# Another opening, another order of small moves and another order of the last stores in a chunked attention kernel with a fused feed-forward

## The chip, the cores and the metric

One core of one Trainium2 chip. The metric is the device time of one execution, in microseconds. Each time is a median or mean over several executions, and what is read from a profile is of one execution; only runs in the fast state (granted TensorE clock 0.993 to 1.00) are compared. In the profile, PE is TensorE's products, PEld its weight loads, DVE is VectorE, ACT is ScalarE, POOL is GpSimd and SP is SyncE, which here only issues transfers.

## The reference

```python
def _attn_ref(q, k, v):                     # each (8, 8, 576, 64), float32
    ...                                     # chunks of 64 positions
    scores = scale * np.matmul(q_c, k_c.transpose(0, 1, 2, 4, 3))
    scores = scores - np.max(scores, axis=-1, keepdims=True)
    attn = np.exp(scores)
    attn = attn / (np.sum(attn, axis=-1, keepdims=True) + 1e-09)
    out = np.matmul(attn, v_c)
    return out.reshape(B, H, S, D)

def _moe_ref(x, w1, w2, w3, w_out):         # x: the attention output as (4608, 512)
    a = x @ w1                              # 512 x 1024
    b = x @ w2
    h = a * b @ w3                          # 1024 x 1024
    return h @ w_out                        # 1024 x 512
```

## The kernel before

The kernel is a list of steps, one letter each, in the order in which they are recorded. A *pair* is 256 tokens (18 pairs in all). For pair p: `q k v` load (GpSimd issues, cast to bf16 on the way), `T` transposes q or k on VectorE, `S` makes scores, `E` is the exponential on ScalarE, `P` the value products, `N` and `X` normalise and transpose on VectorE, `A` and `B` are the products with w1 and w2, `C` copies A's result out on ScalarE, `M` multiplies on VectorE. `V`, `W`, `Z` turn w3 and w_out into one matrix; `O`, `Y`, `Q` are the last product, its copy and its store. `i0` to `i3` are four column pieces of w1 and w2, `o` is w_out, `h0 h1` are the halves of w3. `D` issues products with zeros: `D0.1.4.512` is four of 512 columns. A load such as `q0` is a whole tile of 256 KB in bf16, `q0.0` the half of it with the first half of the heads.

```python
ORDER = """
q0.0 k0.0 q0.1 k0.1 v0 q1.0 q1.1 k1.0 k1.1 i0 v1 q2 k2 i1 v2 i2 i3 q3 k3 v3 o h0 h1 q4 k4 v4
D0.0.32.64 T0.0.0 T0.1.0 T0.0.1 S0.0 T0.1.1 q5 k5 v5 E0.0 S0.1 E0.1 P0.0 P0.1 T1.0.0 N0.0 T1.1.0
...                                          # cut
O16 Y15 Q15 O17 Y16 Q16 Y17 Q17
"""

def do_G(g, a):                              # regroups transposed q and k: qkm <- qkT, 4 moves of 128 KB, 8 for a group
    ...
    for i in (2 * a, 2 * a + 1):
        for e in range(2):
            move(qkm_t[g][blk[2 * a + e], i % 2], qkT_t[g][blk[i], e])

def do_H(g, a):                              # the same for the normalised output: xt <- xm, 64 KB each
    xt = new_xt(g)[:].rearrange("p (s c) -> p s c", s=2)
    for k_ in range(2):
        for i in (2 * a, 2 * a + 1):
            move(xt[blk[2 * a + k_], i % 2], xm_t[g][blk[i], k_].rearrange("p o m t -> p (o m t)"))

def do_O(p):
    if p < NP - 1:
        ...                                  # both halves of the pair; copied by Y, stored by Q
        return
    ...                                      # the last pair: copied and stored in three parts here
```

`move` and the stores are transfers on SyncE's one queue, in program order; `blk[i]` is the i-th group of 32 partitions.

The softmax here doesn't subtract the row's maximum and nothing guards it: scores larger than these inputs give would overflow.

Of the kernel before, what the change touches and what calls it, by code (L numbers as in the profile page):

```python
# [7 lines left out]

ORDER = """
q0.0 k0.0 q0.1 k0.1 v0 q1.0 q1.1 k1.0 k1.1 i0 v1 q2 k2 i1 v2 i2 i3 q3 k3 v3 o h0 h1 q4 k4 v4  # L10
D0.0.32.64 T0.0.0 T0.1.0 T0.0.1 S0.0 T0.1.1 q5 k5 v5 E0.0 S0.1 E0.1 P0.0 P0.1 T1.0.0 N0.0 T1.1.0
T1.0.1 S1.0 T1.1.1 q6 k6 v6 E1.0 X0.0 S1.1 N0.1 X0.1 P1.0 E1.1 T2.0 A0.0 T2.1 q7 k7 B0.0 C0.0 P1.1
v7 M0.0 A0.1 N1.0 B0.1 C0.1 X1.0 S2 N1.1 E2 M0.1 X1.1 P2 A1.0 N2.0 B1.0 X2.0 C1.0 A1.1 N2.1 B1.1
M1.0 C1.1 X2.1 A2.0 M1.1 B2.0 C2.0 A2.1 M2.0 B2.1 T3.0 C2.1 A0.2 M2.1 B0.2 C0.2 T3.1 q8 k8 v8 A1.2
M0.2 B1.2 C1.2 S3 M1.2 A2.2 E3 B2.2 C2.2 P3 M2.2 A0.3 N3.0 B0.3 X3.0 C0.3 A1.3 N3.1 B1.3 M0.3 C1.3
X3.1 A2.3 M1.3 B2.3 C2.3 A3.0 M2.3 B3.0 V0 C3.0 A3.1 M3.0 B3.1 V1 C3.1 A3.2 M3.1 B3.2 C3.2 V2 A3.3
M3.2 B3.3 C3.3 V3 W0 M3.3 T4.0 W1 Z0 V4 V5 T4.1 q9 k9 v9 W2 Z1 V6 V7 T5.0 S4 Z2 W3 T5.1 q10 k10 E4
T6.0 T6.1 P4 v10 q11 k11 Z3 S5 N4.0 O0 E5 X4.0 N4.1 X4.1 T7.0 O1 T7.1 Y0 Q0 T8.0 P5 v11 q12 k12 Y1
S6 T8.1 O2 Q1 E6 N5.0 X5.0 N5.1 X5.1 O3 T9.0 T9.1 Y2 G4.0 P6 v12 q13 k13 A4.0 N6.0 B4.0 G4.1 Y3 X6.0
N6.1 C4.0 A4.1 X6.1 B4.1 C4.1 M4.0 Q2 S7 Q3 M4.1 A4.2 E7 T10.0 B4.2 C4.2 T10.1 P7 v13 q14 k14 A4.3  # L20
M4.2 B4.3 N7.0 C4.3 A4.4 X7.0 M4.3 B4.4 C4.4 N7.1 A4.5 M4.4 B4.5 C4.5 X7.1 S8 M4.5 S9 E8 A4.6 T11.0
B4.6 E9 T11.1 P8 v14 q15 k15 C4.6 A4.7 M4.6 G5.0 B4.7 C4.7 N8.0 A6.0 M4.7 B6.0 N8.1 C6.0 G5.1 A6.1
X8.0 B6.1 M6.0 C6.1 X8.1 P9 v15 q16 k16 A6.2 M6.1 N9.0 B6.2 C6.2 N9.1 A6.3 M6.2 B6.3 C6.3 X9.0 A6.4
M6.3 B6.4 C6.4 X9.1 A6.5 T12.0 H4.0 B6.5 C6.5 M6.4 A6.6 M6.5 B6.6 T12.1 H4.1 C6.6 S10 S11 M6.6 E10
A6.7 T13.0 B6.7 E11 P10 v16 q17 k17 T13.1 C6.7 O4 M6.7 G6.0 N10.0 N10.1 X10.0 G6.1 P11 v17 Y4 X10.1
O5 N11.0 N11.1 Q4 X11.0 X11.1 T14.0 A8.0 H5.0 Y5 B8.0 T14.1 C8.0 A8.1 M8.0 B8.1 H5.1 C8.1 T15.0 A8.2
B8.2 M8.1 C8.2 T15.1 Q5 A8.3 B8.3 C8.3 M8.2 G7.0 S12 M8.3 S13 E12 A8.4 T16.0 B8.4 E13 G7.1 P12 T16.1
C8.4 A8.5 B8.5 M8.4 C8.5 N12.0 A8.6 M8.5 B8.6 C8.6 N12.1 A8.7 M8.6 B8.7 C8.7 X12.0 P13 M8.7 A10.0
X12.1 B10.0 C10.0 N13.0 A10.1 M10.0 B10.1 N13.1 C10.1 A10.2 X13.0 B10.2 M10.1 C10.2 X13.1 S14 S15
M10.2 E14 A10.3 H6.0 T17.0 B10.3 E15 P14 T17.1 C10.3 A10.4 H6.1 M10.3 B10.4 C10.4 N14.0 A10.5 M10.4  # L30
B10.5 G8.0 C10.5 N14.1 A10.6 M10.5 B10.6 C10.6 X14.0 P15 G8.1 X14.1 A10.7 M10.6 B10.7 N15.0 C10.7 O6
N15.1 M10.7 X15.0 X15.1 H7.0 S16 Y6 S17 O7 E16 E17 H7.1 P16 Y7 O8 Q6 N16.0 Q7 N16.1 X16.0 X16.1 P17
Y8 A12.0 N17.0 Q8 B12.0 N17.1 C12.0 A12.1 X17.0 B12.1 M12.0 C12.1 X17.1 A12.2 M12.1 H8.0 B12.2 C12.2
A12.3 M12.2 B12.3 C12.3 H8.1 A12.4 M12.3 B12.4 C12.4 A12.5 M12.4 B12.5 C12.5 A12.6 M12.5 B12.6 C12.6
A12.7 M12.6 B12.7 C12.7 O9 M12.7 O10 Y9 Q9 A14.0 Y10 B14.0 C14.0 Q10 A14.1 M14.0 B14.1 C14.1 A14.2
M14.1 B14.2 C14.2 A14.3 M14.2 B14.3 C14.3 A14.4 M14.3 B14.4 C14.4 A14.5 M14.4 B14.5 C14.5 A14.6
M14.5 B14.6 C14.6 A14.7 M14.6 B14.7 C14.7 O11 M14.7 O12 Y11 Q11 A16.0 Y12 B16.0 C16.0 Q12 A16.1
M16.0 B16.1 C16.1 A16.2 M16.1 B16.2 C16.2 A16.3 M16.2 B16.3 C16.3 A16.4 M16.3 B16.4 C16.4 A16.5
M16.4 B16.5 C16.5 A16.6 M16.5 B16.6 C16.6 A16.7 M16.6 B16.7 C16.7 O13 M16.7 O14 Y13 Q13 O15 Y14 Q14
O16 Y15 Q15 O17 Y16 Q16 Y17 Q17  # L40
"""


# [1 line left out]
def kernel(  # L45
# [11 lines left out]
    nc = tc.nc  # L57
    B, H, S, D = q.shape
    P = 128
    BL = 32  # L60
    NB = P // BL
    CH = 64
# [14 lines left out]
    bf = mybir.dt.bfloat16  # L77
    f32 = mybir.dt.float32
# [4 lines left out]
    io = ctx.enter_context(tc.tile_pool(name="io", bufs=2))  # L83
    asb = ctx.enter_context(tc.tile_pool(name="asb", bufs=2))
    msb = ctx.enter_context(tc.tile_pool(name="msb", bufs=2))
    ps = ctx.enter_context(tc.tile_pool(name="ps", bufs=4, space=bass.MemoryType.PSUM))

    def inorder(ins):
        tc.keep_in_program_order(ins)
        return ins  # L90
# [35 lines left out]
    qk_t = {}  # L126

    HH = H // 2

    def heads(h):  # L130
        return slice(0, H) if h is None else slice(h * HH, (h + 1) * HH)

# [29 lines left out]
    blk = [slice(i * BL, (i + 1) * BL) for i in range(NB)]  # L162
    qkT_t, qkm_t, s_t, e_t, pv_t, xn_t, xm_t, xt_t = {}, {}, {}, {}, {}, {}, {}, {}
# [4 lines left out]
    def move(dst, src):  # L168
        inorder(nc.sync.dma_start(dst, src))
# [11 lines left out]
    def do_G(g, a):  # L181

        if a == 0:
            qkm_t[g] = asb.tile([P, 2, 2, 2, H, CH], bf, tag="qkm", bufs=2, name="qkm")
        for i in (2 * a, 2 * a + 1):
            for e in range(2):
                move(qkm_t[g][blk[2 * a + e], i % 2], qkT_t[g][blk[i], e])

    def do_S(p, hh=None):
        g, m = divmod(p, 2)  # L190
# [50 lines left out]
    def new_xt(g):  # L241

        if g not in xt_t:
            xt_t[g] = asb.tile([P, KO * GT], bf, tag="xt", bufs=4, name="xt")
        return xt_t[g]
# [18 lines left out]
    def do_H(g, a):  # L264

        xt = new_xt(g)[:].rearrange("p (s c) -> p s c", s=2)
        for k_ in range(2):
            for i in (2 * a, 2 * a + 1):
                move(xt[blk[2 * a + k_], i % 2], xm_t[g][blk[i], k_].rearrange("p o m t -> p (o m t)"))

    ab_t, ps_t, a_t, o_t = {}, {}, {}, {}

# [115 lines left out]
    def load_half3(i):  # L388
# [5 lines left out]



    do = {"q": load_q, "k": load_k, "v": load_v, "i": load_w12, "o": load_wo, "h": load_half3, "T": do_T, "S": do_S, "E": do_E, "G": do_G, "H": do_H,
          "P": do_P, "N": do_N, "X": do_X, "A": do_A, "B": do_B, "C": do_C, "M": do_M, "D": do_D, "V": do_V,
          "W": do_W, "Z": do_Z, "O": do_O, "Y": do_Y, "Q": do_Q}
    for step in ORDER.split():  # L400
# [31 lines left out]
```

## Time and profile before

| | before |
|---|---|
| median | 250.58 us |
| span in the profile | 249.3 us |
| TensorE busy | 226.9 us |
| first product with w1 starts | 19.48 us |
| VectorE's last copy starts | 244.40 us |

The page gives busy times as shares of the span, then one digit of busy tenths per fortieth of it; the chain that ended last is followed back from the last instruction. The lines on which the argument stands are in the prediction below. The first load stream in stretches of 3 us (stretch, its length, then PE, PEld, DVE, ACT and POOL busy with counts, granted clock, DMA share, GB/s), of the kernel before:

```profile
6.00:9.00 3.00, 1.08 (x64) 0.94 (x64) 2.19 (x3) 0.60 (x1) 3.00 (x6) 1.00 1.77 130
9.00:12.00 3.00, 1.23 (x80) 0.90 (x72) 0.78 (x2) 0.60 (x1) 3.00 (x5) 1.00 1.64 158
12.00:15.00 3.00, 0.56 (x32) 0.50 (x32) 2.09 (x5) 0.00 (x0) 2.58 (x5) 1.00 1.38 156
```

### The profile page before, as it was taken

To read this page: it belongs to the slowest core of one execution; us is meant where nothing else is said; L and a number is where in the kernel's file an instruction comes from. 1 tells how busy PE (TensorE), PEld (TensorE's weight loads), DVE (VectorE), ACT (ScalarE), POOL (GpSimd) and SP (SyncE) were. 2 spreads that over 40 slices of the span, in tenths; PEclk is the share of its full clock that TensorE was granted. 3 is DMA by queue.
4 is the path that set the end of the run, shared out by engine and by line. 5 is a ranking of instruction groups with operands and counts; after the bars stand their busy time and mean duration, and the time that the engine had idled before them with its cause. 6 is when DMAs were issued, how large, how long until landed. Compare 5 with 4: busy or idle time off the path is not lost.

```text
span 249.3 us, 6372 instructions
## 1 busy us (share of the span) xinstructions
PE 226.9 (91%) x2740; PEld 122.0 (49%) x2760; DVE 154.5 (62%) x236; ACT 83.4 (33%) x116; POOL 86.9 (35%) x116
## 2 busy tenths in 40 slices
PE   3328899999999999999999999999999999999992
PEld 2225688874455445444444444444444444444441
DVE  2566965899879588999998798918440331233000
ACT  2110324332343333535335325262332332331322
POOL 8977854486997254573660000000000000000000
PEclk9999999999999999999999999999999999999998
DMA  7999999999999999999999974635502200400334
GB/s 67 145 165 182 193 185 201 196 174 172 155 169 209 221 225 249 177 209 193 204 194 235 271 128 99 147 76 199 151 3 84 84 0 9 162 0 1 139 116 168
DMA packets 93660, 37.12 MB, mean 149 GB/s; under 512 B 77120, under 2 KB 86592, under 8 KB 93632
## 3 DMA queue, kind: packets, MB, share of 16 engines
q0 software_dynamic: 84736, 19.41, 84.6%
q1 hardware_dynamic: 8896, 17.31, 24.0%
q8 instruction: 22, 0.36, 0.6%
q14 instruction: 6, 0.05, 0.1%
HBM read 38.80 MB, written 9.44 MB: 194 GB/s over the span
## 4 chain that ended last, share of the span: by engine, by line
PE 73%; DMA 17%; POOL 3%; DVE 2%; issue 1%; ACT 1%; SPq 0%; DVEq 0%; ACTq 0%; POOLq 0%
PE ab_ps L93 41%; PE o_ps L93 22%; DMA out_dram<-o_sb 6%; DMA w<-in_moe_w_dram 6%; PE w_ps L93 6%; DMA qkm<-qkT 5%; PE s_ps L93 3%; PE pv L93 2%; POOL qk L96 2%; DVE qkT L177 1%; POOL vbuf L96 1%; ACT e L209 0%; DVE ab L321 0%; POOL w L96 0%; ACT a_sb L306 0%
## 5 line engine op out<-in xcount | busy, mean ns | idle before, releaser
L93 PE MATMUL ab_ps<-xt,w 128*128 128x512 bf16 (+1 forms) x697 | 130.0, 343 | 1.1 <-DMA w<-in_moe_w_dram 0.5
L93 PEld LDWEIGHTS <-w 128*128 128x128 bf16 x704 | 67.8, 99 | 55.6 <-DMA w<-in_moe_w_dram 0.9
L321 DVE TENSOR_TENSOR ab<-a_sb,ab_ps 128x512 bf16<-128x512 f32 x72 | 48.9, 679 | 49.3 <-ACT a_sb L306 49.2
L306 ACT COPY a_sb<-ab_ps 128x512 f32<-128x512 f32 x72 | 42.2, 585 | 87.9 <-PE ab_ps L93 85.9
L93 PE MATMUL o_ps<-w3o,ab 128*128 128x512 bf16 (+1 forms) x285 | 63.3, 373 | 0.6
L177 DVE STREAM_TRANSPOSE qkT<-qk 128x1024 bf16<-128x1024 bf16 (+1 forms) x40 | 45.6, 1178 | 11.0 <-DMA qk<-in_q_dram 8.3
L93 PEld LDWEIGHTS <-ab 128*128 128x128 bf16 x296 | 28.5, 98 | 32.2
L96 POOL DMA_DIRECT2D vbuf<-in_v_dram x40 | 33.8, 854 | 14.6 <-DMA qk<-in_q_dram 6.4
L351 ACT COPY o_sb<-o_ps 128x1024 f32<-128x1024 f32 x17 | 17.2, 1012 | 42.8 <-PE o_ps L93 38.8
L239 DVE TENSOR_TENSOR xn<-pv,rc 128x512 bf16<-128x512 f32 x36 | 24.9, 692 | 1.2
L96 POOL DMA_DIRECT2D qk<-in_k_dram x26 | 20.2, 782 | 10.0 <-DMA vbuf<-in_v_dram 7.3
L96 POOL DMA_DIRECT2D qk<-in_q_dram x26 | 20.3, 788 | 8.2 <-DMA qk<-in_k_dram 2.3
L209 ACT ACTIVATE e<-s_ps 128x1024 bf16<-128x1024 f32 (+1 forms) x18 | 17.1, 978 | 8.9 <-PE s_ps L93 8.7
L93 PE MATMUL pv<-vbuf,e 64*32 64x65 bf16 (+1 forms) x832 | 11.0, 200 | 4.5 <-DMA vbuf<-in_v_dram 3.3
L93 PE MATMUL w_ps<-wo,w3T 128*128 128x512 bf16 x62 | 14.0, 379 | 0.1
L93 PEld LDWEIGHTS <-e 64*32 64x32 bf16 (+1 forms) x832 | 8.3, 99 | 11.5 <-issue 6.6
L236 DVE RECIPROCAL rc<-pv 128x8 f32<-128x8 f32 x36 | 6.9, 192 | 11.3 <-PE pv L93 11.2
L96 POOL DMA_DIRECT2D w<-in_moe_w_dram x16 | 11.1, 696 | 7.4 <-DMA wo<-in_moe_w_out_dram 3.4
L259 DVE STREAM_TRANSPOSE xm<-xn 128x512 bf16<-128x512 bf16 x20 | 13.6, 697 | 0.2
L251 DVE STREAM_TRANSPOSE xt<-xn 128x512 bf16<-128x512 bf16 x16 | 11.3, 707 | 0.4
L93 PEld LDWEIGHTS <-qkT 32*64 32x64 bf16 x512 | 5.8, 116 | 11.2 <-DVE qkT L177 9.2
L344 DVE COPY o_sb<-o_ps 128x256 f32<-128x256 f32 x1 | 0.4, 424 | 16.0 <-PE o_ps L93 16.0
(19 smaller groups left out, 45.4 us busy)
## 6 DMA issues: line engine op xcount, KB each, us to landing
out_dram<-o_sb SPq DMA_DIRECT2D x17, 512.0 KB, 2.9
qkm<-qkT SPq DMA_DIRECT2D x40, 128.0 KB, 7.2
vbuf<-in_v_dram POOLq DMA_DIRECT2D x32, 128.0 KB, 8.7
w<-in_moe_w_dram POOLq DMA_DIRECT2D x16, 256.0 KB, 10.0
qk<-in_q_dram POOLq DMA_DIRECT2D x10, 256.0 KB, 8.3
qk<-in_k_dram POOLq DMA_DIRECT2D x10, 256.0 KB, 10.1
xt<-xm SPq DMA_DIRECT2D x40, 64.0 KB, 3.0
qk<-in_q_dram POOLq DMA_DIRECT2D x8, 128.0 KB, 5.1
```

Of the source, the lines that this page charges most:

```text
L93: return inorder(nc.tensor.matmul(*a, **kw))
L96: return inorder(nc.gpsimd.dma_start(dst, src))
L177: inorder(nc.vector.transpose(qkT_t[g][:, :, p % 2, s, heads(h)].rearrange("p e h (y t) -> p h t e y", t=2), qk_t[p][:, s, heads(h)].rearr ...
L209: inorder(nc.scalar.activation(e_t[p][:, :, heads(hh)], s_t[p][:].rearrange("p u (h q) -> p u h q", q=CH)[:, :, heads(hh)], Exp, scale=sca ...
L236: inorder(nc.vector.reciprocal(rc[:], pv[:, :, :, D:W]))
L239: inorder(nc.vector.tensor_mul(xn_t[p][:, u], pv[:, :, :, 0:D], rc.to_broadcast([P, 2, 4, D])))
L251: inorder(nc.vector.transpose(new_xt(g)[:].rearrange("p (o t) -> p o t", o=KO)[:, :, t0:t0 + UT] .rearrange("p o (m y) -> p m o y", y=BL), ...
L259: inorder(nc.vector.transpose(xm_t[g][:, u, :, m].rearrange("p o (c y) -> p c o y", y=BL), xn_t[p][:].rearrange("p u r m d -> p (u r) m d" ...
L306: inorder(nc.scalar.copy(a_t[p, j][:], ps_t[p, j][:, 0, :]))
L321: inorder(nc.vector.tensor_mul(o, view(a_t.pop((p, j))[:]), view(ps_t.pop((p, j))[:, 1, :])))
L344: inorder(copy(o_sb[:, u, n0:n1], t[:, 0, 0:n1 - n0]))
L351: inorder(nc.scalar.copy(o_sb[:], ps_t.pop(p)[:]))
```

## The change

Its intent: TensorE's first expert products earlier and at the rate of the later ones (110 ns each instead of 205); the small moves spread over both halves of the partitions; the big store of pair 16 out of the way of the very last one. `R` loads half of pair 0's q as fp32 on the queue of SyncE or of ScalarE (the two hardware queues of the prediction), and `K` casts it on ScalarE; all other loads up to pair 4 are whole tiles now.

```diff
 ORDER:
-q0.0 k0.0 q0.1 k0.1 v0 q1.0 q1.1 k1.0 k1.1 i0 v1 q2 k2 i1 v2 i2 i3 q3 k3 v3 o h0 h1 q4 k4 v4
-D0.0.32.64 T0.0.0 T0.1.0 T0.0.1 S0.0 T0.1.1 ...
+R0 R1 k0 v0 q1 i0 k1 v1 i1 i2 q2 k2 v2 i3 q3 k3 v3 q4 k4 v4 o h0 h1 D0.0.16.64 K0 K1 T0.0 T0.1 q5 k5
+v5 S0 T1.0 E0 P0 D0.1.4.512 T1.1 q6 k6 v6 N0.0 S1 D1.0.5.512 X0.0 N0.1 X0.1 A0.0 E1 B0.0 C0.0 P1
 ... (A to M of pairs 0 to 3 in another order; scores of pair 4 ahead of A3.0)
-O16 Y15 Q15 O17 Y16 Q16 Y17 Q17
+O16 Y15 Q15 Y16 Q16 O17

+    def do_R(h):
+        raw_t[h] = msb.tile([P, HH, 2 * D], f32, tag="o_sb", name="raw")
+        inorder((nc.sync, nc.scalar)[h].dma_start(raw_t[h][:], q[0, heads(h), 0:4 * CH, :]...))
+    def do_K(h):
+        ...
+        inorder(nc.scalar.copy(qk_t[0][:, 0, heads(h)], raw_t[h][:]))

 do_G:
-        for i in (2 * a, 2 * a + 1):
-            for e in range(2):
-                move(qkm_t[g][blk[2 * a + e], i % 2], qkT_t[g][blk[i], e])
+        for i in (0, 2, 1, 3):
+            e = (i + a) % 2
+            move(qkm_t[g][blk[i // 2 * 2 + e], i % 2], qkT_t[g][blk[i], e])
 do_H: likewise
```

More of the change, by code (lines that the diff above doesn't have):

```diff
@@ L9 @@
 ORDER = """
-q0.0 k0.0 q0.1 k0.1 v0 q1.0 q1.1 k1.0 k1.1 i0 v1 q2 k2 i1 v2 i2 i3 q3 k3 v3 o h0 h1 q4 k4 v4
-D0.0.32.64 T0.0.0 T0.1.0 T0.0.1 S0.0 T0.1.1 q5 k5 v5 E0.0 S0.1 E0.1 P0.0 P0.1 T1.0.0 N0.0 T1.1.0
-T1.0.1 S1.0 T1.1.1 q6 k6 v6 E1.0 X0.0 S1.1 N0.1 X0.1 P1.0 E1.1 T2.0 A0.0 T2.1 q7 k7 B0.0 C0.0 P1.1
-v7 M0.0 A0.1 N1.0 B0.1 C0.1 X1.0 S2 N1.1 E2 M0.1 X1.1 P2 A1.0 N2.0 B1.0 X2.0 C1.0 A1.1 N2.1 B1.1
-M1.0 C1.1 X2.1 A2.0 M1.1 B2.0 C2.0 A2.1 M2.0 B2.1 T3.0 C2.1 A0.2 M2.1 B0.2 C0.2 T3.1 q8 k8 v8 A1.2
@@ L15 @@
-M0.2 B1.2 C1.2 S3 M1.2 A2.2 E3 B2.2 C2.2 P3 M2.2 A0.3 N3.0 B0.3 X3.0 C0.3 A1.3 N3.1 B1.3 M0.3 C1.3
-X3.1 A2.3 M1.3 B2.3 C2.3 A3.0 M2.3 B3.0 V0 C3.0 A3.1 M3.0 B3.1 V1 C3.1 A3.2 M3.1 B3.2 C3.2 V2 A3.3
-M3.2 B3.3 C3.3 V3 W0 M3.3 T4.0 W1 Z0 V4 V5 T4.1 q9 k9 v9 W2 Z1 V6 V7 T5.0 S4 Z2 W3 T5.1 q10 k10 E4
-T6.0 T6.1 P4 v10 q11 k11 Z3 S5 N4.0 O0 E5 X4.0 N4.1 X4.1 T7.0 O1 T7.1 Y0 Q0 T8.0 P5 v11 q12 k12 Y1
-S6 T8.1 O2 Q1 E6 N5.0 X5.0 N5.1 X5.1 O3 T9.0 T9.1 Y2 G4.0 P6 v12 q13 k13 A4.0 N6.0 B4.0 G4.1 Y3 X6.0
@@ L20 @@
-N6.1 C4.0 A4.1 X6.1 B4.1 C4.1 M4.0 Q2 S7 Q3 M4.1 A4.2 E7 T10.0 B4.2 C4.2 T10.1 P7 v13 q14 k14 A4.3
-M4.2 B4.3 N7.0 C4.3 A4.4 X7.0 M4.3 B4.4 C4.4 N7.1 A4.5 M4.4 B4.5 C4.5 X7.1 S8 M4.5 S9 E8 A4.6 T11.0
-B4.6 E9 T11.1 P8 v14 q15 k15 C4.6 A4.7 M4.6 G5.0 B4.7 C4.7 N8.0 A6.0 M4.7 B6.0 N8.1 C6.0 G5.1 A6.1
-X8.0 B6.1 M6.0 C6.1 X8.1 P9 v15 q16 k16 A6.2 M6.1 N9.0 B6.2 C6.2 N9.1 A6.3 M6.2 B6.3 C6.3 X9.0 A6.4
-M6.3 B6.4 C6.4 X9.1 A6.5 T12.0 H4.0 B6.5 C6.5 M6.4 A6.6 M6.5 B6.6 T12.1 H4.1 C6.6 S10 S11 M6.6 E10
@@ L25 @@
-A6.7 T13.0 B6.7 E11 P10 v16 q17 k17 T13.1 C6.7 O4 M6.7 G6.0 N10.0 N10.1 X10.0 G6.1 P11 v17 Y4 X10.1
-O5 N11.0 N11.1 Q4 X11.0 X11.1 T14.0 A8.0 H5.0 Y5 B8.0 T14.1 C8.0 A8.1 M8.0 B8.1 H5.1 C8.1 T15.0 A8.2
-B8.2 M8.1 C8.2 T15.1 Q5 A8.3 B8.3 C8.3 M8.2 G7.0 S12 M8.3 S13 E12 A8.4 T16.0 B8.4 E13 G7.1 P12 T16.1
-C8.4 A8.5 B8.5 M8.4 C8.5 N12.0 A8.6 M8.5 B8.6 C8.6 N12.1 A8.7 M8.6 B8.7 C8.7 X12.0 P13 M8.7 A10.0
-X12.1 B10.0 C10.0 N13.0 A10.1 M10.0 B10.1 N13.1 C10.1 A10.2 X13.0 B10.2 M10.1 C10.2 X13.1 S14 S15
@@ L30 @@
-M10.2 E14 A10.3 H6.0 T17.0 B10.3 E15 P14 T17.1 C10.3 A10.4 H6.1 M10.3 B10.4 C10.4 N14.0 A10.5 M10.4
-B10.5 G8.0 C10.5 N14.1 A10.6 M10.5 B10.6 C10.6 X14.0 P15 G8.1 X14.1 A10.7 M10.6 B10.7 N15.0 C10.7 O6
-N15.1 M10.7 X15.0 X15.1 H7.0 S16 Y6 S17 O7 E16 E17 H7.1 P16 Y7 O8 Q6 N16.0 Q7 N16.1 X16.0 X16.1 P17
-Y8 A12.0 N17.0 Q8 B12.0 N17.1 C12.0 A12.1 X17.0 B12.1 M12.0 C12.1 X17.1 A12.2 M12.1 H8.0 B12.2 C12.2
-A12.3 M12.2 B12.3 C12.3 H8.1 A12.4 M12.3 B12.4 C12.4 A12.5 M12.4 B12.5 C12.5 A12.6 M12.5 B12.6 C12.6
@@ L35 @@
-A12.7 M12.6 B12.7 C12.7 O9 M12.7 O10 Y9 Q9 A14.0 Y10 B14.0 C14.0 Q10 A14.1 M14.0 B14.1 C14.1 A14.2
-M14.1 B14.2 C14.2 A14.3 M14.2 B14.3 C14.3 A14.4 M14.3 B14.4 C14.4 A14.5 M14.4 B14.5 C14.5 A14.6
-M14.5 B14.6 C14.6 A14.7 M14.6 B14.7 C14.7 O11 M14.7 O12 Y11 Q11 A16.0 Y12 B16.0 C16.0 Q12 A16.1
-M16.0 B16.1 C16.1 A16.2 M16.1 B16.2 C16.2 A16.3 M16.2 B16.3 C16.3 A16.4 M16.3 B16.4 C16.4 A16.5
-M16.4 B16.5 C16.5 A16.6 M16.5 B16.6 C16.6 A16.7 M16.6 B16.7 C16.7 O13 M16.7 O14 Y13 Q13 O15 Y14 Q14
-O16 Y15 Q15 O17 Y16 Q16 Y17 Q17
+R0 R1 k0 v0 q1 i0 k1 v1 i1 i2 q2 k2 v2 i3 q3 k3 v3 q4 k4 v4 o h0 h1 D0.0.16.64 K0 K1 T0.0 T0.1 q5 k5
@@ new lines @@
+v5 S0 T1.0 E0 P0 D0.1.4.512 T1.1 q6 k6 v6 N0.0 S1 D1.0.5.512 X0.0 N0.1 X0.1 A0.0 E1 B0.0 C0.0 P1
+M0.0 A0.1 N1.0 X1.0 B0.1 C0.1 N1.1 A0.2 X1.1 B0.2 C0.2 M0.1 A1.0 T2.0 B1.0 C1.0 M0.2 A1.1 T2.1 q7 k7
+v7 B1.1 C1.1 M1.0 S2 M1.1 A0.3 E2 T3.0 B0.3 C0.3 P2 M0.3 A1.2 N2.0 X2.0 B1.2 C1.2 N2.1 A1.3 X2.1
+B1.3 C1.3 M1.2 A2.0 T3.1 q8 k8 v8 B2.0 C2.0 M1.3 S3 T4.0 A2.1 E3 M2.0 B2.1 T4.1 q9 k9 C2.1 P3 v9
+M2.1 A2.2 N3.0 B2.2 C2.2 X3.0 A2.3 N3.1 B2.3 X3.1 C2.3 M2.2 S4 M2.3 A3.0 E4 B3.0 C3.0 A3.1 M3.0 B3.1
+C3.1 V0 A3.2 M3.1 B3.2 C3.2 V1 A3.3 M3.2 B3.3 C3.3 V2 W0 M3.3 V3 W1 Z0 V4 V5 W2 Z1 V6 V7 T5.0 Z2 W3
@@ new lines @@
+T5.1 q10 k10 T6.0 T6.1 P4 v10 q11 k11 Z3 S5 N4.0 O0 E5 X4.0 N4.1 X4.1 T7.0 O1 T7.1 Y0 Q0 T8.0 P5 v11
+q12 k12 Y1 S6 T8.1 O2 Q1 E6 N5.0 X5.0 N5.1 X5.1 O3 T9.0 T9.1 Y2 G4.0 P6 v12 q13 k13 A4.0 N6.0 B4.0
+G4.1 Y3 X6.0 N6.1 C4.0 A4.1 X6.1 B4.1 C4.1 M4.0 Q2 S7 Q3 M4.1 A4.2 E7 T10.0 B4.2 C4.2 T10.1 P7 v13
+q14 k14 A4.3 M4.2 B4.3 N7.0 C4.3 A4.4 X7.0 M4.3 B4.4 C4.4 N7.1 A4.5 M4.4 B4.5 C4.5 X7.1 S8 M4.5 S9
+E8 A4.6 T11.0 B4.6 E9 T11.1 P8 v14 q15 k15 C4.6 A4.7 M4.6 G5.0 B4.7 C4.7 N8.0 A6.0 M4.7 B6.0 N8.1
@@ new lines @@
+C6.0 G5.1 A6.1 X8.0 B6.1 M6.0 C6.1 X8.1 P9 v15 q16 k16 A6.2 M6.1 N9.0 B6.2 C6.2 N9.1 A6.3 M6.2 B6.3
+C6.3 X9.0 A6.4 M6.3 B6.4 C6.4 X9.1 A6.5 T12.0 H4.0 B6.5 C6.5 M6.4 A6.6 M6.5 B6.6 T12.1 H4.1 C6.6 S10
+S11 M6.6 E10 A6.7 T13.0 B6.7 E11 P10 v16 q17 k17 T13.1 C6.7 O4 M6.7 G6.0 N10.0 N10.1 X10.0 G6.1 P11
+v17 Y4 X10.1 O5 N11.0 N11.1 Q4 X11.0 X11.1 T14.0 A8.0 H5.0 Y5 B8.0 T14.1 C8.0 A8.1 M8.0 B8.1 H5.1
+C8.1 T15.0 A8.2 B8.2 M8.1 C8.2 T15.1 Q5 A8.3 B8.3 C8.3 M8.2 G7.0 S12 M8.3 S13 E12 A8.4 T16.0 B8.4
@@ new lines @@
+E13 G7.1 P12 T16.1 C8.4 A8.5 B8.5 M8.4 C8.5 N12.0 A8.6 M8.5 B8.6 C8.6 N12.1 A8.7 M8.6 B8.7 C8.7
+X12.0 P13 M8.7 A10.0 X12.1 B10.0 C10.0 N13.0 A10.1 M10.0 B10.1 N13.1 C10.1 A10.2 X13.0 B10.2 M10.1
+C10.2 X13.1 S14 S15 M10.2 E14 A10.3 H6.0 T17.0 B10.3 E15 P14 T17.1 C10.3 A10.4 H6.1 M10.3 B10.4
+C10.4 N14.0 A10.5 M10.4 B10.5 G8.0 C10.5 N14.1 A10.6 M10.5 B10.6 C10.6 X14.0 P15 G8.1 X14.1 A10.7
+M10.6 B10.7 N15.0 C10.7 O6 N15.1 M10.7 X15.0 X15.1 H7.0 S16 Y6 S17 O7 E16 E17 H7.1 P16 Y7 O8 Q6
+N16.0 Q7 N16.1 X16.0 X16.1 P17 Y8 A12.0 N17.0 Q8 B12.0 N17.1 C12.0 A12.1 X17.0 B12.1 M12.0 C12.1
@@ new lines @@
+X17.1 A12.2 M12.1 H8.0 B12.2 C12.2 A12.3 M12.2 B12.3 C12.3 H8.1 A12.4 M12.3 B12.4 C12.4 A12.5 M12.4
+B12.5 C12.5 A12.6 M12.5 B12.6 C12.6 A12.7 M12.6 B12.7 C12.7 O9 M12.7 O10 Y9 Q9 A14.0 Y10 B14.0 C14.0
+Q10 A14.1 M14.0 B14.1 C14.1 A14.2 M14.1 B14.2 C14.2 A14.3 M14.2 B14.3 C14.3 A14.4 M14.3 B14.4 C14.4
+A14.5 M14.4 B14.5 C14.5 A14.6 M14.5 B14.6 C14.6 A14.7 M14.6 B14.7 C14.7 O11 M14.7 O12 Y11 Q11 A16.0
+Y12 B16.0 C16.0 Q12 A16.1 M16.0 B16.1 C16.1 A16.2 M16.1 B16.2 C16.2 A16.3 M16.2 B16.3 C16.3 A16.4
@@ L41 @@
+M16.3 B16.4 C16.4 A16.5 M16.4 B16.5 C16.5 A16.6 M16.5 B16.6 C16.6 A16.7 M16.6 B16.7 C16.7 O13 M16.7
+O14 Y13 Q13 O15 Y14 Q14 O16 Y15 Q15 Y16 Q16 O17
 """
@@ L128 @@
     HH = H // 2
+    raw_t = {}
+    def do_R(h):
+        raw_t[h] = msb.tile([P, HH, 2 * D], f32, tag="o_sb", name="raw")
+        inorder((nc.sync, nc.scalar)[h].dma_start(
+            raw_t[h][:], q[0, heads(h), 0:4 * CH, :].rearrange("h (p t) d -> p h (t d)", t=2)))
+    def do_K(h):
+        if 0 not in qk_t:
+            qk_t[0] = io.tile([P, 2, H, 2 * D], bf, tag="qk", bufs=5, name="qk")
+        inorder(nc.scalar.copy(qk_t[0][:, 0, heads(h)], raw_t[h][:]))
     def heads(h):
@@ L266, in do_H @@
         xt = new_xt(g)[:].rearrange("p (s c) -> p s c", s=2)
-        for k_ in range(2):
-            for i in (2 * a, 2 * a + 1):
-                move(xt[blk[2 * a + k_], i % 2], xm_t[g][blk[i], k_].rearrange("p o m t -> p (o m t)"))
+        for i in (0, 2, 1, 3):
+            move(xt[blk[i // 2 * 2 + a], i % 2], xm_t[g][blk[i], a].rearrange("p o m t -> p (o m t)"))
     ab_t, ps_t, a_t, o_t = {}, {}, {}, {}
@@ L390, in load_half3 @@
         load_w3(i * n, (i + 1) * n)
-    do = {"q": load_q, "k": load_k, "v": load_v, "i": load_w12, "o": load_wo, "h": load_half3, "T": do_T, "S": do_S, "E": do_E, "G": do_G, "H": do_H,
+    do = {"q": load_q, "k": load_k, "v": load_v, "i": load_w12, "o": load_wo, "h": load_half3, "T": do_T, "S": do_S, "R": do_R, "K": do_K, "E": do_E, "G": do_G, "H": do_H,
           "P": do_P, "N": do_N, "X": do_X, "A": do_A, "B": do_B, "C": do_C, "M": do_M, "D": do_D, "V": do_V,
```

## The prediction

The forecast's sum is 1.7 us for the opening, 0.5 for the moves and 1.2 for the stores, 3.4 together: 250.7 - 3.4 = 247.3 us. Zero products should quicken the products after them and moves in another order should land sooner; the up to 1.5 us for the first, inside the opening, and the 0.5 us for the second are estimates. The 427 ns of a zero product of 512 columns is twice the 213 or 214 ns between the starts of the slow products of 256 in before's trace. That the hardware queues can begin at about 0.8 us is an estimate too, from the first instructions of ScalarE (0.73 us) and VectorE (0.86 us) there. The share of 1.7 to 1.8 is that of the transfer engines in before, from 6 to 24.65 us.

> **What bounds the kernel now.** I read the page's slices first, then busy time in chosen stretches, the chain that ended last, and last the instructions of the first 60 us and of the end in order of time. The slices (one digit is 6.2 us):
>
> ```profile
> PE   3328899999999999999999999999999999999992
> DVE  2566965899879588999998798918440331233000
> PEclk9999999999999999999999999999999999999998
> DMA  7999999999999999999999974635502200400334
> ```
>
> TensorE is loosely filled for four slices, full for 35, nearly empty in the last. The transfer engines are full from the second slice to the 23rd. So time can come only from the opening, the tail, or small holes between. Busy time of each engine in six stretches (the columns are stretch, length, then PE, PEld, DVE, ACT and POOL busy with counts, granted clock, DMA share, GB/s):
>
> ```profile
> 0.00:6.00 6.00, 1.89 (x32) 1.73 (x32) 1.43 (x8) 1.28 (x1) 4.96 (x10) 1.00 0.68 66
> 6.00:12.00 6.00, 2.31 (x128) 1.84 (x128) 2.97 (x5) 1.19 (x2) 6.00 (x9) 1.00 1.70 144
> 12.00:18.00 6.00, 1.39 (x74) 1.23 (x76) 4.72 (x9) 1.19 (x2) 4.43 (x7) 1.00 1.71 161
> 18.00:24.65 6.65, 5.33 (x88) 3.59 (x86) 3.54 (x5) 0.58 (x1) 5.05 (x7) 1.00 1.79 181
> ...
> 171.00:244.40 73.40, 73.10 (x373) 33.92 (x376) 19.56 (x30) 23.67 (x35) 0.00 (x0) 1.00 0.21 73
> 244.40:249.30 4.90, 0.00 (x0) 0.00 (x0) 0.42 (x1) 0.36 (x1) 0.00 (x0) 0.82 0.53 191
> ```
>
> In the first 24.65 us TensorE is busy 10.9 us, 1.9 of them with zero products. From 171 to the end of its work it idles 0.3 us; after 244.40 it does nothing for 4.9 us. The chain agrees: it leaves the weight transfers for TensorE at 24.65 us.
>
> ```profile
> 9.72 7.24 DMA w<-in_moe_w_dram
> 16.96 0.28 issue
> 17.24 7.36 DMA w<-in_moe_w_dram
> 24.61 0.05 issue
> 24.65 1.05 PE ab_ps L93 x8
> ```
>
> The instructions in order of time show what the early products cost (start, duration, then what), here the first 16 products of 256 columns and, later, 112 of them:
>
> ```profile
> 19.48 3.28 PE L93 MATMUL ab_ps<-xt,w 128*128 128x256 bf16 x16
> ...
> 42.33 12.40 PE L93 MATMUL ab_ps<-xt,w 128*128 128x256 bf16 x112
> ```
>
> 205 ns against 110 ns each: the first group costs 1.5 us too much.
>
> [...] its share of 1.7 to 1.8 while loading says that the engines are the limit. [...] Before moves the regrouped q and k (qkm) first wholly in the lower half, then in the upper; 128 KB land in about 7.1 us. [...]
>
> **The change part by part.**
>
> *q of pair 0 on two hardware queues.* Removed: two GpSimd issues of about 0.8 us (0.89 and 0.77). Loading whole instead of half tiles removes three more (k of pair 0, q and k of pair 1), together about 3.9 us of issue. Added: two fp32 loads and two ScalarE casts of 128x512, about 0.6 us each by the row of a_sb copies (585 ns), while ScalarE idles. The bytes read from memory are the same, and GpSimd's issues at 9 us were already some 0.5 MB ahead of what had moved (ten 128 KB issues of q, k and v against 6 x 66 + 3 x 130 GB/s = 0.79 MB), so only the start is gained: the hardware queues can begin at about 0.8 us, against 1.24 plus 0.89 of issue. My estimate is that the whole load stream runs 1.2 us earlier.
>
> *Weight piece 0 ahead of k of pair 1, pieces 1 and 2 ahead of pair 2.* Landings before, as issue start plus time to landing: k of pair 1 about 14.3, weight piece 0 15.6 and 16.96, v of pair 1 17.9 and 19.1, piece 1 23.2 and 24.6. The set up to k of pair 1 plus piece 0 is unchanged, so its last member, now k, lands at 16.96 - 1.2 = 15.8. Then VectorE: transpose of k 1.3, two rounds of normalise and transpose at 1.6 each (reciprocal 0.2, product 0.69, transpose 0.7) = 20.3. So the first expert product starts at 20.5, a microsecond later than the 19.48 of before. But it finds piece 1 landed (24.6 less 3.0 for pair 2's q and k less 1.2 = 20.4) and piece 2 at about 23[...]. From 20.5 I lay TensorE's groups (16 products of 256 columns = 1.76; scores 0.64; value products 0.63): piece 0 to 22.4 [...], value products to 23.1, pieces 1 and 2 of pair 0 to 26.6, pieces 0 and 1 of pair 1 (transposes ready 26.9) to 30.4, pair 2's scores after VectorE at 30.8 to 31.4. Done by then: three scores, two value groups, five piece groups = 1.92 + 1.26 + 8.8 = 12.0 us of work. Before had three scores, three value groups and four piece groups less two products, 10.7 us, at 31.62. Gain about 1.5 us. Later waits of 0.3 us shrink: 1.5 to 1.9.
>
> *Zero products in waits.* 9 of 512 columns, 427 ns each [...], 3.8 us in all, in stretches where TensorE waits for k and for VectorE. The five ahead of the first expert product end at about 20.5, beside the chain. Their worth, up to 1.5 us, is counted above.
>
> *q, k, v of pair 4 ahead of the last two weights; scores of pair 4 earlier.* Before, the first half of w3 lands at 36.52 + 10.8 = 47.3, and VectorE starts its transposes (V) at 49.00. Pair 4 in front costs about 4.4 us (pair 3 took from 31.8 to 36.2), less 1.2: 50.5. The new order puts V one group later, and pair 4's scores (0.64) in front; with the gain it is wanted at 49.3 to 49.5. So VectorE waits about 1 us there. The weight product needs two V and one evacuation, 3.05 us after landing: 53.6, where TensorE is ready at 53.5. So the load stream caps the gain: 1.7 us is kept here (before: 54.73 + 0.64 for the scores = 55.4).
>
> *Moves of qkm and xt in another order.* Same count and bytes, alternating between the halves of the partitions. In 86 to 150 us TensorE idles 1.8 us, of which 1.2 is waits for qkm transfers and 0.5 "issue" within pair scores. I give 0.5.
>
> *Stores at the end.* Before, the copy of pair 16 stands behind pair 17's:
>
> ```profile
> 242.64 0.59 ACT L344 COPY o_sb<-o_ps 128x512 f32<-128x512 f32 x1 [4.17 <-PE o_ps L93]
> 243.25 2.41 SPq L169 DMA_DIRECT2D out_dram<-o_sb  x4
> 243.47 0.37 ACT L344 COPY o_sb<-o_ps 128x256 f32<-128x256 f32 x1 [0.24 <-PE o_ps L93]
> 243.74 1.02 ACT L351 COPY o_sb<-o_ps 128x1024 f32<-128x1024 f32 x1
> 244.40 0.42 DVE L344 COPY o_sb<-o_ps 128x256 f32<-128x256 f32 x1 [16.04 <-PE o_ps L93]
> ```
>
> Its 512 KB are issued last, at 245.3, and land 2.8 us later, 248.1. Now the copy runs at about 240.9 under pair 17's products, and the last store is 128 KB at 244.9, landing at 246.9 (2.0, a little above its 1.8). Gain 1.2 us.
>
> Sum: 1.7 + 0.5 + 1.2 = 3.4; 250.7 - 3.4 = 247.3 us.
>
> **The rivals.** First, w3 arrives later still: a stall of 3 us at the weight product eats the opening, and only tail and moves remain, 1.7 us, 249.0. For it: GpSimd waits for earlier transfers before nearly every weight issue from 28 to 44 us[...]. Against: the author moved V back by one group. Second, the load stream starts faster than I allow, since the first six microseconds move only 66 GB/s; 2.5 us there lifts the cap too, and with an idle-free middle and tail gives about 245.5. Third, the zero products [...] delay the first product: 1 us worse, 248.3. Fourth, VectorE, 90% busy from 86 to 150, cannot follow an earlier TensorE; its work moves with the opening, so I expect at most 0.5 us of it.
>
> **Range and chances.** The tail is nearly certain (0.9 to 1.5), the opening 0 to 3, the moves 0 to 1.2. Predicted 247.3 us, range 245.5 to 249.1. Over 2% faster is below 245.7, which needs the opening and the moves both at their best: 0.13. Within 2%: 0.85. Slower by over 2%: 0.02.
>
> **What would show it.** Right: first expert product at 20 to 21 us at about 110 to 120 ns each; VectorE waiting for w at its first V near 50 us; the weight product starting near 53.6; last store landing about 2 us after TensorE ends, and 3.8 us rather than 4.9 from there to the span's end. Wrong: k of pair 1 landing before 14 us (load stream faster), the weight product after 55 (w3 too late), score waits for qkm in 86 to 150 unchanged, or new VectorE waits there.

## The result, and the profile after

A ratio here is the mean time of one kernel's fast runs over the mean of the other's fast runs of the same rounds, so it is not quite the ratio of the medians quoted beside it.

| | changed, median | before, median | ratio, 95% interval |
|---|---|---|---|
| first runs | 247.83 us | 250.58 us | 0.9874, 0.9835 to 0.9913 |
| second set | 246.21 us | 251.32 us | 0.9799, 0.9757 to 0.9841 |
| third set | 246.44 us | 250.93 us | 0.9809, 0.9764 to 0.9855 |

The times lie inside the predicted range of 245.5 to 249.1 us. The later sets are better than the first and than the predicted 247.3, near the 2% mark and not clearly on either side of it. The changed kernel's profiled run fell in the slow state in the first two sets (granted clock 0.768, 305.02 us; and 0.952, 253.33 us). Those two and a third, not profiled (249.91 us at 0.991, third set), are left out of all comparisons; the profile read here is of the third set, 245.16 us at clock 1.00. So 3 of 16 runs of the changed kernel were slow, and none of 37 runs of before nor of 58 of the variants below.

The slices of the changed kernel:

```profile
PE   1459999999999999999999999999999999999994
```

TensorE (one digit is 6.1 us) is full from the fourth slice on. The stretches that answer to those of before (the last two here are the stretch to the end of TensorE's work and the rest):

```profile
6.00:12.00 6.00, 2.76 (x131) 1.97 (x132) 3.38 (x3) 1.02 (x1) 5.54 (x8) 1.00 1.77 177
12.00:18.00 6.00, 3.39 (x71) 1.51 (x69) 3.74 (x7) 1.02 (x1) 3.43 (x6) 1.00 1.80 183
18.00:24.65 6.65, 6.65 (x110) 5.18 (x109) 3.34 (x7) 1.17 (x2) 4.44 (x7) 1.00 1.80 179
...
171.00:240.20 69.20, 68.98 (x328) 31.80 (x326) 16.09 (x25) 22.44 (x33) 0.00 (x0) 1.00 0.20 70
240.20:243.30 3.10, 0.00 (x0) 0.00 (x0) 0.30 (x1) 0.00 (x0) 0.00 (x0) 1.00 0.38 132
```

From 6 to 12 us the transfers move 177 GB/s where they moved 144, and from 18 to 24.65 us TensorE has no hole (two of 0.3 us follow, at 25.64 and 36.35). The chain that ended last (start, duration, what), at its beginning:

```profile
6.32 7.78 DMA qk<-in_k_dram
14.10 0.02 issue
14.12 1.32 DVE qkT L188
15.44 0.04 issue
15.49 5.61 PE z_ps L92 x68
```

No longer a weight but pair 1's k is the transfer that the opening waits for; it lands at 14.1 us. In order of time, the first expert products, VectorE's first transpose of w3, and the end of the changed kernel:

```profile
18.59 2.50 PE L92 MATMUL z_ps<-xt,w 128*128 128x256 bf16 x16
...
50.68 1.25 DVE L373 STREAM_TRANSPOSE w3T<-w 128x1024 bf16<-128x1024 bf16 x1 [1.50 <-DMA w<-in_moe_w_dram]
...
52.91 13.98 PE L92 MATMUL w_ps<-wo,w3T 128*128 128x512 bf16 x64
...
236.59 1.01 ACT L362 COPY o_sb<-o_ps 128x1024 f32<-128x1024 f32 x1 [2.44 <-PE o_ps L92]
240.07 0.42 DVE L355 COPY o_sb<-o_ps 128x256 f32<-128x256 f32 x1 [16.04 <-PE o_ps L92]
```

Bracketed is the idle time before an instruction and what ended it. Pair 16's copy now stands at 236.59 us, 3.5 us ahead of the last copy instead of beside it.

Where the time went can be read at two points that both kernels have: the start of pair 4's value products, before which lies everything that the opening changes (each kernel has then done the same products), and the start of VectorE's last copy.

| profile of | start to pair 4's value products | to the last copy | to the end of the span |
|---|---|---|---|
| before | 69.22 | 175.18 | 4.90 |
| changed | 66.82 | 173.25 | 3.23 |
| difference | -2.40 | -1.93 | -1.67 |

The profiled run is a fast one of its set, so the sum, -6.0, is more than the 4.8 us between the means of that set (246.38 and 251.19).

### The profile page after: what moved, and what is told of

Same layout as the page of the kernel before. It is cut to its first block, busy times and chain, and to the rows that moved or that the text cites. A ratio compares the mean times of both kernels' runs of the same rounds, so it can differ in the third digit from the quotient of the medians.

```text
span 303.2 us, 6345 instructions
## 1 busy us (share of the span) xinstructions
PE 286.6 (94%) x2731; PEld 136.0 (45%) x2753; DVE 155.9 (51%) x232; ACT 84.3 (28%) x116; POOL 83.7 (28%) x111
## 4 chain that ended last, share of the span: by engine, by line
PE 93%; DMA 3%; POOL 2%; issue 1%; DVE 1%; DVEq 0%; POOLq 0%
PE ab_ps L92 53%; PE o_ps L92 27%; PE w_ps L92 6%; PE pv L92 3%; DMA qk<-in_k_dram 3%; PE s_ps L92 2%; PE z_ps L92 2%; POOL qk L95 1%; POOL vbuf L95 1%; POOL w L95 0%; DVE qkT L188 0%; DVE o_sb L355 0%; DVEq L355 0%; POOLq L428 0%
## 5 line engine op out<-in xcount | busy, mean ns | idle before, releaser
L92 PE MATMUL ab_ps<-xt,w 128*128 128x512 bf16 (+1 forms) x681 | 163.6, 411 | 0.8
L92 PEld LDWEIGHTS <-w 128*128 128x128 bf16 x704 | 77.7, 113 | 79.6 <-issue 70.4
L92 PE MATMUL o_ps<-w3o,ab 128*128 128x512 bf16 (+1 forms) x285 | 82.1, 453 | 1.1
L92 PEld LDWEIGHTS <-ab 128*128 128x128 bf16 x296 | 32.5, 111 | 46.8 <-issue 45.3
L188 DVE STREAM_TRANSPOSE qkT<-qk 128x1024 bf16<-128x1024 bf16 x36 | 45.0, 1286 | 8.7 <-ACT qk L139 4.1
L95 POOL DMA_DIRECT2D qk<-in_k_dram x24 | 19.1, 804 | 4.1 <-DMA w<-in_moe_w_dram 2.0
L95 POOL DMA_DIRECT2D qk<-in_q_dram x23 | 18.1, 793 | 5.3 <-DVE qkT L188 1.5
L92 PE MATMUL w_ps<-wo,w3T 128*128 128x512 bf16 x62 | 18.0, 460 | 0.3 <-issue 0.3
L221 ACT ACTIVATE e<-s_ps 128x1024 bf16<-128x1024 f32 x16 | 15.9, 1026 | 1.0 <-PE s_ps L92 0.6
L92 PEld LDWEIGHTS <-w3T 128*128 128x128 bf16 x64 | 7.1, 110 | 10.8 <-issue 10.7
```

The lines of the kernel that those rows point to most:

```text
L92: return inorder(nc.tensor.matmul(*a, **kw))
L95: return inorder(nc.gpsimd.dma_start(dst, src))
L188: inorder(nc.vector.transpose(qkT_t[g][:, :, p % 2, s, heads(h)].rearrange("p e h (y t) -> p h t e y", t=2), qk_t[p][:, s, heads(h)].rearr ...
L221: inorder(nc.scalar.activation(e_t[p][:, :, heads(hh)], s_t[p][:].rearrange("p u (h q) -> p u h q", q=CH)[:, :, heads(hh)], Exp, scale=sca ...
```

## The experiments

Three calls of four kernels each, the first two on one chip and the third on another; the kernel before ran 11 times in each. The three columns are read as above, from one profile each; the times are those of 5 or 6 runs. Single profiles are uncertain by half a microsecond or so: the first three openings of 69.22, 69.56 and 69.68 us, of before and of the two kernels with its opening, are the same work.

| kernel | opening | middle | tail | median | ratio to before |
|---|---|---|---|---|---|
| stores only | 69.56 | 175.76 | 3.28 | 249.16 | 0.9922 (0.988 to 0.9963) |
| moves only | 69.68 | 173.69 | 4.83 | 249.77 | 0.9948 (0.9907 to 0.999) |
| opening only | 66.80 | 176.16 | 4.74 | 249.01 | 0.9912 (0.9872 to 0.9951) |
| changed, old moves | 67.36 | 175.60 | 3.14 | 246.84 | 0.9834 (0.9806 to 0.9862) |
| changed, no zero products | 69.20 | 173.87 | 3.23 | 246.39 | 0.9841 (0.9805 to 0.9877) |
| changed, q by GpSimd | 66.54 | 173.91 | 3.35 | 245.93 | 0.9811 (0.9785 to 0.9838) |
| changed, more zero products | 67.16 | 173.50 | 3.14 | 245.73 | 0.9798 (0.9774 to 0.9822) |
| changed, k ahead of piece 0 | 66.16 | 174.69 | 3.15 | 244.95 | 0.9761 (0.9727 to 0.9794) |
| changed, w3 ahead of pair 4 | 66.97 | 174.83 | 3.20 | 246.96 | 0.9827 (0.9792 to 0.9862) |
| changed, both | 67.07 | 175.17 | 3.16 | 245.91 | 0.9801 (0.9759 to 0.9844) |

**The changed kernel again**, twice, with no edit.

> The changed kernel once more, for a profile at full clock and a narrower ratio. Both theories: 246.5 to 248 us in the fast state, last store landing about 2 us after TensorE ends, TensorE's work shifted by about 1.7 to 2 us earlier. Theory of the prediction (three separate gains: opening 1.7, moves 0.5, tail 1.2): VectorE waits for w at its first V near 50 us. Rival (the opening gives nothing, because w3 lands late): the weight product starts after 55 us.

> The changed kernel again beside its variants, for a profile at full clock. Both theories: 245.5 to 247 us; k of pair 1 lands at 14 to 15 us, first expert product at 18.5 to 19.5 us.

Measured: 246.21 and 246.44 us. The weight product starts at 52.91 us, so the rival "the opening gives nothing" is out.

**The three parts alone.** Edits: in the kernel before, only the line of the last stores; in the kernel before, only the loops of `do_G` and `do_H`; in the changed kernel, both of these put back.

> Before with nothing changed but the copy and store of pair 16 set ahead of pair 17. Theory of the prediction: 1.2 us faster, from a last store of 128 KB in place of 512 KB. Rival (the end is fixed work after the last store, or the stores share bandwidth): under 0.4 us.

> Before with nothing changed but the order of the qkm and xt moves. Theory of the prediction: landing of qkm falls from 7.1 us to under 5, the score waits for qkm (about 1.2 us from 86 to 150 us) go, 0.5 us faster. Rival (other things fill those holes): landing falls but the time stays within 0.2 us.

> The changed kernel with the old order of moves and the old order of the last stores: only the new opening is left. Theory of the prediction: 1.7 us faster than before. Rival 1 (w3 in the way): 0 to 0.5 us. Rival 2 (the opening is worth all of the measured 3 us): 2.5 us or more.

The product of the three ratios is 0.9922 x 0.9948 x 0.9912 = 0.9784, and the whole change had 0.9799: the parts add up within the intervals. Each part touches its own column of the table: the stores the tail (4.90 to 3.28), the moves the middle (175.18 to 173.69), the opening the first (69.22 to 66.80). The expectation of under 5 us for one qkm move failed over all forty moves: the median landing fell only from 7.2 to 6.6 us. It held in the one group for which TensorE waits, the eight moves ahead of pair 14's scores: 7.2 to 4.2 us (6.2 in the changed kernel). SyncE's issues (start, time over all, what, count) of that group, in before and in moves only:

```profile
136.77 7.63 SPq L169 DMA_DIRECT2D qkm<-qkT  x8
```

```profile
136.71 5.55 SPq L169 DMA_DIRECT2D qkm<-qkT  x8
```

What held the last move back in before is in the chain to pair 14's scores:

```profile
136.13 7.74 DMA out_dram<-o_sb
143.89 4.94 DMA qkm<-qkT
```

SyncE issued the last of the eight moves only when the store of 512 KB, eight transfers before it, had landed: it waited 1.5 us for it. The move landed at 148.83 us; TensorE had reached the scores at 148.34. In moves only the store landed in 5.5 us, the last move was issued at 141.68 and landed at 144.17. The loads that ran beside this group were lighter there, though (0.20 MB against 0.55 in its first 7.5 us; 0.43 in the changed kernel), and the other four groups show no clear change, so how much of it is the order was not separated. With the new order TensorE has no wait for qkm left (0.7 us in before). The waits of TensorE between 60 and 240 us (who waited for what: us in total, times, longest) in opening only and in moves only:

```profile
PE s_ps L92 <- DMA qkm<-qkT: 1.6, 2, 1.4
PE s_ps L92 <- issue: 0.6, 1, 0.6
```

```profile
PE s_ps L93 <- issue: 0.6, 1, 0.6
```

Opening only pays more for the old moves than before did (1.6 us against 0.7 in this view): TensorE reaches pair 14's scores 2.4 us earlier (145.96 against 148.34 us), while the last of their moves lands only 1.4 us earlier (147.46 against 148.83). That is where part of the opening's 2.4 us went in that kernel; its middle is 1.0 us longer than that of before.

**The changed kernel with the old moves.**

> The changed kernel with the old order of qkm and xt moves. The first four runs showed that with the new opening and the old moves TensorE waits 1.4 us at one pair score (near 146 us). Theory (the moves matter more once TensorE is earlier, because that wait is set by the store queue and not by TensorE): this wait of 1 us or more returns, and the kernel is 1.3 to 2 us slower than the changed kernel, so 0.984 to 0.988 of before. Rival (moves are a small extra): within 0.6 us of the changed kernel.

Measured: a wait of 1.3 us for qkm is back, in two pieces; the middle is 175.60 against 173.25 us. The timed loss is less than expected: means of 246.89 against 246.16 and 246.38 in the other two calls, 0.5 to 0.7 us, with intervals that overlap. That the wait returns is shown; the size that I expected, 1.3 us or more, is not, and the rival's 0.6 us is about met.

**Without the zero products of 512 columns.** Edit:

```diff
-P0 D0.1.4.512 T1.1 ... S1 D1.0.5.512 X0.0
+P0 T1.1 ... S1 X0.0
```

> The changed kernel without the nine zero products of 512 columns; the sixteen short ones at the start stay. Theory [...]: the first 16 expert products take 3.2 to 3.4 us in place of 2.7 and some later ones stay slow, 0.7 to 1.5 us slower in all. Rival (they only occupy a wait, and the five ahead of the first product delay it): the same time or up to 0.3 us faster.

**With more of them.** Edit:

```diff
-D0.1.4.512 ... D1.0.5.512
+D0.1.13.512 ... D1.0.6.512
```

> The changed kernel with 13 instead of 4 zero products after the first value group, and 6 instead of 5 ahead of the first expert product, so that TensorE is busy without a gap from about 10 us. Theory [...]: the first 16 expert products take about 1.8 us in place of 2.7, 0.7 to 1 us faster. Rival (the products overshoot and delay the scores of pair 1): the same time or slower.

The first 16 expert products in order of time, without any and with more:

```profile
19.45 3.37 PE L92 MATMUL ab_ps<-xt,w 128*128 128x256 bf16 x16 [2.13 <-DVE xt L263]
```

```profile
19.60 1.91 PE L92 MATMUL z_ps<-xt,w 128*128 128x256 bf16 x16 [0.99 <-DVE xt L263]
```

211 against 119 ns each: the zero products do set the rate of these products. The column of the granted clock shows 1.00 both without any (19.4 to 23 us) and in the changed kernel (18 to 24.65 us). With the changed kernel's nine, 2.50 us in the run above, 2.70 in opening only, 2.64 with the old moves, 1.91 with q by GpSimd and with w3 first. The traces show what is in between: the starts of the products are 213 or 214 ns apart up to some product and 109 after it. Without zero products all 16 are slow, with more of them none; with the nine it is five to seven in three kernels, and none in two; the zero products themselves start 427 ns apart or 216. Why the switch falls where it does, these runs don't show. In time, the mean without them is 246.86 us, against 246.13 and 245.78 for the two other kernels of that call, and 246.16 and 246.38 for the changed kernel in the other calls: a loss of 0.5 to 1.1 us that is likely, but whose intervals overlap. (The 69.20 in the table overstates it: that profiled run, 248.04 us, has a hole of 1.4 us in pair 2's value products with nothing in the trace to wait for.) More of them ties with the changed kernel within the intervals, 0.9798 against 0.9799 and 0.9809: the theory had the rate right and the time wrong. Their first expert product starts at 19.60 us, a microsecond later than in the changed kernel.

**Pair 0's q by GpSimd.** Edit:

```diff
-R0 R1 k0 v0 ... K0 K1 T0.0
+q0 k0 v0 ... T0.0
```

> The changed kernel with pair 0's q loaded as one whole tile by GpSimd with its cast, no hardware load and no ScalarE casts. Theory (the hardware load starts the stream early): k of pair 1 lands 1 us or more later, the first expert product starts near 19.5 to 20 us in place of 18.7, and the kernel is 0.8 to 1.3 us slower. Rival (the engines are the limit and only the first scores move): k of pair 1 lands within 0.4 us of before, time within 0.3 us.

The rival was right in the time. The load stream of this kernel, in the stretches shown for before:

```profile
6.00:9.00 3.00, 0.28 (x20) 0.28 (x24) 2.55 (x2) 0.00 (x0) 3.00 (x5) 1.00 2.16 166
9.00:12.00 3.00, 1.87 (x125) 1.39 (x118) 1.32 (x1) 1.02 (x1) 3.00 (x4) 1.00 1.56 192
12.00:15.00 3.00, 1.50 (x4) 0.30 (x2) 0.38 (x1) 0.00 (x0) 1.49 (x4) 1.00 1.96 173
```

Pair 1's k lands at 14.6 us, inside the 14.0 to 15.1 us of the kernels with the hardware load, and the time is the same: 246.13 us against 246.16 and 246.38. So the two hardware queues, first in the change's list, are not what makes the opening faster: they add to the stream only up to 6 us. From 3 to 6 us it moves 213 GB/s with them (q as fp32 is twice the bytes) and 133 without, in the three stretches after that 163, 192, 172 with them and 166, 192, 173 without. Before moved 130, 158, 156 GB/s in the same three, with no hardware load either. What differs between these two is that whole tiles replace halves (four GpSimd issues fewer up to pair 1's k) and that a weight piece comes earlier. The kernel with k first, below, has k ahead of that piece as before does, and its stream is as fast:

```profile
6.00:9.00 3.00, 0.51 (x38) 0.51 (x42) 2.20 (x2) 0.00 (x0) 3.00 (x5) 1.00 2.09 166
9.00:12.00 3.00, 1.87 (x110) 1.31 (x99) 1.62 (x2) 1.02 (x1) 2.19 (x4) 1.00 1.61 185
```

So the earlier piece isn't needed either. What both have and before lacks is whole tiles: GpSimd takes 0.89 to 1.01 us to issue 256 KB of q or k as one tile, and 0.76 to 0.89 us for a half of 128 KB, by my estimate from these numbers some 145 to 170 GB/s at most. So whole tiles are the likely cause, by elimination: before with nothing changed but them was not run, and that the hardware loads would do in the one kernel and the earlier piece in the other is not excluded.

**Pair 1's k ahead of weight piece 0; w3 ahead of pair 4; both.** Edits:

```diff
-q1 i0 k1 v1                    # k first
+q1 k1 i0 v1
-q4 k4 v4 o h0 h1               # w3 first; T4, S4, E4 go back behind V3 to T5 as before
+o h0 h1 q4 k4 v4
```

> The changed kernel with pair 1's k loaded ahead of weight piece 0 instead of behind it. Theory (the landing of pair 1's k gates VectorE and so the first expert product): k lands about 2 us earlier, first product near 16.5 us; but the w3 transposes then wait for w3, which lands no earlier, so at most 1 us of it reaches the end: 0 to 1 us faster than the changed kernel. Rival (weight piece 0 then gates): first product within 0.5 us of the changed kernel's.

> The changed kernel with w_out and w3 loaded ahead of pair 4 again, and pair 4's transposes and scores where they stood before. Theory (w3's landing is close but not binding in the changed kernel): VectorE no longer waits for w at its first V, and the time is the same within 0.4 us. Rival (w3's landing caps the opening, as the prediction had it): 0.5 us or more faster.

> Both of these together. Theory: with w3 out of the way the earlier first product reaches the end, 1 to 2 us faster than the changed kernel, and more than k first alone. Rival (other arrivals, weight pieces 1 to 3 and pair 2, then gate): no faster than k first alone.

The kernel with k first, in order of time:

```profile
16.17 0.81 PE L92 MATMUL z_ps<-xt,w 128*128 128x256 bf16 x6
...
29.75 1.05 PE L92 MATMUL ab_ps<-xt,w 128*128 128x256 bf16 x8 [1.01 <-DMA w<-in_moe_w_dram]
...
36.05 1.92 PE L92 MATMUL ab_ps<-xt,w 128*128 128x256 bf16 x16 [1.03 <-DVE xt L263]
...
52.25 13.98 PE L92 MATMUL w_ps<-wo,w3T 128*128 128x512 bf16 x64
```

The first product is 2.4 us earlier, as the theory has it: pair 1's k is the gate. But weight piece 3 (1.0 us, and 0.3 just before) and pair 3's q, which holds VectorE and through it pair 2's transposes (1.0 us), take most of it back, and the weight product is only 0.66 us earlier. With w3 first, VectorE's wait for w is gone (48.51 us, no wait) and nothing is gained: the opening is 66.97 us against 66.82, the mean time 246.87 against 246.38 (its middle has a wait of 1.1 us for xt that the changed kernel lacks). With both, 246.18 us: the theory of 1 to 2 us failed and the rival was right, other arrivals gate. (There too the middle has a wait of 1.1 us, for qkm.)

K first has the lowest median of all, 244.95 us, and its interval lies wholly below 0.98. Against the changed kernel it is 245.16 to 246.38 us in the mean, 0.5% faster; the two intervals to before overlap, so that it beats before is shown and that it beats the changed kernel is only likely.

## Why the prediction was right or wrong

The range and the direction were right; all three terms were too small in the profile and several reasons were wrong. The first set's gain, 3.2 us in the means, lies near the predicted 3.4, but the later sets gained 5.1 and 4.8: that near hit is luck and supports no term.

- *The opening, 1.7 us.* Measured 2.4 us in the profile and 2.3 us (251.26 less 248.99) in the means of opening only. The first failing step: "GpSimd's issues at 9 us were already some 0.5 MB ahead of what had moved ... so only the start is gained". The count was right and the conclusion was not: the rate rose from 144 to 177 GB/s between 6 and 12 us, pair 1's k landed at 14.1 instead of 15.8, the first expert product began at 18.59 instead of 20.5. The reading that a share of 1.7 to 1.8 means that the engines are the limit failed with it: in that stretch 144 GB/s went with 1.70, and 177 with 1.77. The second rival, a load stream faster than I allowed, is the one that came true, if not by its full 2.5 us.
- *The hardware queues* as the source of "1.2 us earlier" fell: without them nothing is lost (246.13 us against 246.16 and 246.38).
- *The cap by w3.* VectorE did wait for w at its first V, 1.5 us at 50.68, where I had about 1 us near 50.5. But "the load stream caps the gain" was wrong: TensorE had products queued through that wait and none of it reached the weight product (52.91, predicted 53.6), and taking the wait away gained nothing.
- *The zero products.* That they quicken the first products was right (119 ns each with more of them, 211 with none), by what mechanism these runs don't show; the opening's working let the first group run nearly at the later rate (20.5 to 22.4 for it), and it took 2.50 us, 156 ns each instead of 110 to 120, with 0.3 us lost twice behind VectorE's transposes later (25.64 and 36.35 us). From first product to weight product it took 34.3 us against the 33.0 of my working, which gave back some of the earlier start.
- *The moves, 0.5 us.* The holes in 86 to 150 us went, 1.8 us to 0.4, and the middle shrank by 1.5 us alone and 1.9 in the whole. The failing step is the term's size: I took less than half of the holes that I had listed. In time, moves only gained 1.3 us, but taking the moves out of the changed kernel cost only 0.5 to 0.7. The mechanism that I gave, quicker landings, is seen in the one group that counts and not over all forty moves; the group was issued 2.1 us sooner because the store ahead of it landed sooner. That the halves of the partitions are the reason was not shown.
- *The stores, 1.2 us.* Measured 1.6 in stores only, 1.8 in time. The order of events was as told. The two sizes that were off are those of the last store: it is issued 0.45 us after the last copy starts, not 0.5, and lands in 1.70 us, not 2.0. From the last landing to the end of the span it is 1.11 us in both kernels. SyncE's waits for stores at the very end fell from 2.2 to 1.1 us.
- *The fourth rival*, VectorE unable to follow from 86 to 150 us, did not show.
- *The chance of 0.13* for over 2% may have been low: two sets came out at 0.9799 and 0.9809, neither clear of the mark.

Open: whether whole tiles alone, put into before, raise the early rate; how much of the moves' gain is their order; why only the changed kernel had slow runs; the spread between the sets (0.9874 against 0.9799); the hole called "issue" in TensorE's scores or value products (0.3 to 1.4 us, in some runs).

## What to carry to other kernels

A share of busy transfer engines that looks full is not yet a limit (here 1.70 at 144 GB/s and 1.77 at 177): look at the rate, at the issuing engine in the same stretch and at the bytes of each issue before concluding that issues cost nothing. Look for what gates the first dense work in order of arrival, because moving one gate can uncover the next (here k, then weight piece 3 and pair 3's q, 1.0 us each). And when one stage is made earlier, list the transfers further on whose time is set by other transfers and not by that stage, since they may be waited for there (here the waits for qkm grew from 0.7 to 1.6 us).
